# Attention with a mixture-of-experts layer behind it on one Trainium2 core: the same instructions in the order of another scheduler

## The chip, the cores and the metric

The kernel runs on one core of one Trainium2 chip. A core has five engines, each with a queue of its own that it works off strictly in order: TensorE (PE in the profile; its weight loads PEld), VectorE (DVE), ScalarE (ACT), GpSimd (POOL) and SyncE (SP), which here only issues transfers. ACT and POOL issue a few transfers too. The engines wait for each other through semaphores. The metric is the time of one execution on the device in microseconds (us), the median of several runs.

## The reference

```python
scores = scale * np.matmul(q, k.transpose(0, 1, 3, 2))        # 8 batches x 8 heads, 576 positions, 64 dims
mask = block_i >= block_j                                      # causal in blocks of 64
scores = np.where(mask, scores, -1000000000.0)
attn = np.exp(scores - np.max(scores, axis=-1, keepdims=True))
attn = attn / (np.sum(attn, axis=-1, keepdims=True) + 1e-09)
out = np.matmul(attn, v)
x = out.transpose(0, 2, 1, 3).reshape(B * S, H * D)            # 4608 tokens x 512
h = x @ w_in                                                   # 512 x 2048
sp = np.maximum(h, 0.0) + np.log1p(np.exp(-np.abs(h)))         # softplus
g = h * erf(sp)
return (g @ w_out).astype(np.float32)                          # 2048 x 512
```

The weights arrive as float64. The kernel works with pairs of float32r (or float16) numbers, a high and a low part, so a product takes three matmuls.

## The kernel before, in words

The work has two parts that share the engines, and a third behind them.

**Attention** goes over 64 heads (eight batches of eight). For each head, `load_qk` issues four transfers and two subtractions: POOL issues the keys and queries into one of four buffers (L307), SP copies them within the buffer (L308, L309), and POOL subtracts to make the low parts (L312, L313). A buffer is free when PE has done the last matmuls of the head four before. PE makes the scores once for the rows' maxima (L324; DVE reduces them at L327, the maxima go back into the buffer through L354 and L356), once more with keys on partitions (L370, L371); ACT takes the exponential (L375) and the float16 high part (L381), DVE the low part (L382). Every two heads PE multiplies by the values (L414) and makes the sums (L437). Every four heads `normalise` divides (L469 on DVE, L470 on ACT, L471 on POOL) and SP stores the result to a DRAM tensor `x_d` (L472).

**The first part of the MoE layer** takes 6 of the 16 chunks of `d_ff` (128 columns each). It runs over 18 tiles of 256 tokens, three units of two chunks a tile: 54 units. A unit's steps are: the first product on PE (L154, called up here, from the loads of x at L187), the gate `h * erf(softplus(h))` as a polynomial of a tanh (ACT L123 and twice L128, DVE three times L130, then L135, ACT L136, POOL L137), and the second product (L164, called down here). A tile's sums are stored to `part_d` (L210). A tile can start when its batch has gone through all its eight heads, so the first tile stands behind head 7's normalisation. Its six weight chunks are converted from float64 words by `load_weight` (transfer L94; DVE L98, L99, L102, L104, L105; ACT L101, L106; POOL L107, L108) during the first heads, and 110 matmuls that feed nothing (`warm`, L510) stand between those heads. Four more chunks of weights go into the four key buffers as these come free at the end (`early_w2`, eight half-chunks, staged in one buffer for the raw words).

**The second part** (the other 10 chunks) goes over tiles of 512 tokens and adds `part_d`.

The steps are issued by a Python loop over the heads; `merge` spreads the lists of steps of one turn evenly over it. `late` shifts the priority of a kind of steps by a number of instructions:

```python
tc.cur_priority += PRIO.get(kind, 0)
f()
tc.cur_priority -= PRIO.get(kind, 0)
PRIO = {"pv": -74, "w1": 400, "w2": -300}
```

The order in which instructions stand in each engine's queue is not the order of the program. The framework's scheduler makes it: each instruction has a priority, by default its place in the program, and the scheduler picks among those that its model holds ready.

Of the kernel before, what the change touches and what calls it, by code (L numbers as in the profile page):

```python
# [15 lines left out]
AX = mybir.AxisListType  # L16
# the top word of the float64 2**-126, read as a float32
LEAST = 0.25 * (1 + 0.125) * 2.0**-13
PSUM = bass.MemoryType.PSUM

# erf(softplus(h)) as a function of r0 = tanh(T0 * h + T1).  Each step makes the next r:
#   ("S", i):    (p[0] * r_i + p[1]) ** 2
#   ("M", i, j): (r_i + p[0]) * r_j
#   ("A", i, j): p[0] * r_i + r_j
# and the value is the last r plus FIN.
PROG = [('S', 0), ('S', 1), ('M', 2, 2), ('M', 1, 3), ('M', 4, 4)]
# [8 lines left out]
def tile_attention_moe(ctx: ExitStack, tc: tile.TileContext, qk, v, w, maskrows, sels, out):  # L35
    nc = tc.nc
# [52 lines left out]
    def load_weight(whi, wlo, stage, f):  # L89
        """the two float32r parts of chunk f of both weights, out of the words of their float64"""  # L90
        for s in range(2):
            nm = f"{f}_{s}"
            raw = stage[0][0].tile([P, stage[0][2]], I32, tag=stage[0][1][s], bufs=stage[0][3], name=f"raw{nm}")[:, : 2 * DM].rearrange("p (n t) -> p n t", t=2)
            nc.sync.dma_start(raw.rearrange("p n t -> p (n t)"), w[f, s].bitcast(I32))  # L94
            top, low = raw[:, :, 1], raw[:, :, 0]
            # sign, exponent and 20 bits of mantissa as a float32 (0 for what is below its range)
            bits = stage[1][0].tile([P, stage[1][2]], I32, tag=stage[1][1], bufs=stage[1][3], name=f"bits{nm}")[:, :DM]
            nc.vector.tensor_scalar(out=bits, in0=top, scalar1=3, scalar2=0x3FFFFFF8, op0=ALU.logical_shift_left, op1=ALU.bitwise_and)  # L98
            nc.vector.scalar_tensor_tensor(out=bits, in0=top, scalar=-0x40000000, in1=bits, op0=ALU.bitwise_and, op1=ALU.bitwise_or)  # L99
            sq = stage[2][0].tile([P, stage[2][2]], F32, tag=stage[2][1], bufs=stage[2][3], name=f"sq{nm}")[:, :DM]  # L100
            nc.scalar.activation(sq, f32(top), AF.Square)  # L101
            nc.vector.scalar_tensor_tensor(out=sq, in0=sq, scalar=LEAST * LEAST, in1=f32(bits), op0=ALU.is_ge, op1=ALU.mult)  # L102
            # the low word, of the weight that the exponent gives it
            nc.vector.tensor_scalar(out=bits, in0=sq.bitcast(I32), scalar1=-0x800000, scalar2=None, op0=ALU.bitwise_and)  # L104
            nc.vector.scalar_tensor_tensor(out=f32(bits), in0=low.bitcast(U32), scalar=2.0**-52, in1=f32(bits), op0=ALU.mult, op1=ALU.mult)  # L105
            nc.scalar.copy(whi[:, s, :], sq)  # L106
            nc.gpsimd.tensor_tensor(out=sq, in0=sq, in1=f32(whi[:, s, :]), op=ALU.subtract)  # L107
            nc.gpsimd.tensor_tensor(out=wlo[:, s, :], in0=sq, in1=f32(bits), op=ALU.add)  # L108
        return whi, wlo
# [3 lines left out]
    def gate(h, name, gpool):  # L113
        """g = h * erf(softplus(h)) as a sum of two float32r parts"""
        n = h.shape[1]
# [27 lines left out]
    def moe_unit(ws, xh, xl, o, tw, nu, u, name, first, last, spread):  # L143
        """nu chunks of d_ff over tw tokens: the steps to their g, and those to their part of o"""
        turns.append(u)
# [25 lines left out]
    def merged(*lists):  # L171
        """the steps of all lists, each list (steps, from, to) spread evenly over its part of the whole"""
        order = []
        for n, (steps, lo, hi) in enumerate(lists):
            order += [(lo + (hi - lo) * (i + 0.5) / len(steps), n, i) for i in range(len(steps))]
        return [lists[n][0][i] for _, n, i in sorted(order)]
# [4 lines left out]

# [1 line left out]
    def load_x(pool, t, tw):  # L183
# [33 lines left out]
    def moe1(ready, lag):  # L217
        """the next step of the first F1 chunks, if there is one: a unit up to its g together with an earlier unit from g on"""
        t = len(xs1)
# [19 lines left out]
    with tc.tile_pool(name="apool", bufs=2) as apool, tc.tile_pool(name="spool", bufs=1) as spool, \  # L239
# [4 lines left out]
        nc.sync.dma_start(sel, sels)  # L244
        # columns of the keys' tiles 0, 3, 4 and 1, 2 in the two parts of a head's probabilities
        p32s = [spool.tile([P, n], F32, name=f"p32_{i}") for i, n in enumerate(PN)]
# [10 lines left out]
        def bank(name):  # L257
            """a bank of PSUM; all of them take part as long as the other chunks of d_ff need none"""
            turn.append(0)
            k = len(turn) % 8 if not xs1 else 0  # L260
            if k in (2, 5):
                return ps_h.tile([P, 512], F32, tag="h", name=name)
            if k in (3,):
                return ps_o.tile([P, 512], F32, tag="o", name=name)
            return ps_a.tile([P, 512], F32, tag="a", name=name)
# [6 lines left out]
        def prep_v(b, qd, v32):  # L272
            """two float16 parts of v over its largest magnitude, and that magnitude"""
            nm = f"{b}_{qd}"
# [21 lines left out]
        def part(n, i):  # L296
            """part i of head n: kl over kh, qh over ql, kh over 5 rows that mask, qh over 5 rows that mask"""
            return qks[n % NB][:, i * S : (i + 1) * S]
# [18 lines left out]
        def maxes(n):  # L317
            """the steps to the rows' maxima, negated, in the row of t that goes with the ones"""
            mx, K = mxs[n % 2], D + 4
# [41 lines left out]
        def probs(n, out):  # L361
            """the steps to exp(0.125 * s - its maximum), keys on partitions, in two float16 parts"""
            K = D + 5
# [25 lines left out]
        def pv(qd, pp, prs, V, usb, rs):  # L389
            """the steps to the unnormalised outputs of heads 2pp and 2pp+1 of the quad, and to their sums"""  # L390
            vsb, vh, vl = V
            st = {}

            def ranges(q0, q1):
                """keys' tiles that a part of the queries attends to: the queries, and where their probabilities are"""
                for j in range(5):
# [21 lines left out]

            # the sums of two heads' first 384 and last 192 queries, in a group of 32 columns each
            order = []  # L420
# [24 lines left out]
        def normalise(b, qd, usbs, rs):  # L445
            nm = f"{b}_{qd}"
            # pair, tile of the sums, part of the queries, head
            ri = apool.tile([P, 2, 3, 2, 2], F32, tag="ri", name=f"ri{nm}")
# [36 lines left out]
        def late(kind, steps):  # L485
            """steps whose instructions the scheduler holds behind the next ones of the order, or ahead of some (offsets in instructions)"""
            def run(f):
# [69 lines left out]

# [1 line left out]
    N2 = 2  # L559
# [89 lines left out]
```

## Time and profile before

| what | value |
| --- | --- |
| median of 3 runs | 1394.77 us |
| lowest and highest run | 1393.82 and 1400.65 us |
| span of the profiled execution | 1407.0 us |
| mean granted TensorE clock in it | 0.951 |
| busy PE, DVE, ACT, POOL | 1273.8, 1013.9, 793.2, 602.1 us |
| moved by DMA | 179.95 MB |

The profiled execution is one execution of its own, 12.2 us above the median of the runs. An engine counts as busy while it executes an instruction; matmuls are pipelined, and a busy PE is not a PE at its peak. "Idle before" in a group of instructions is the time that the engine stood idle just before them, with the event that ended it behind the arrow. In a timeline each row gives the start, the duration, the engine, the line of the code and the operands; the idle time in front of it stands in brackets.

### The profile page before, as it was taken

The page shows a single profiled execution, that of the slowest core. Times are in us where ns is not written, and L with a number is a line of the kernel's source. Part 1 is how long each engine was busy: PE and PEld are TensorE (multiplying, and loading weights), DVE is VectorE, ACT ScalarE, POOL GpSimd, SP SyncE. Part 2 cuts the span into 40 slices and gives each one's busy share as a digit, 9 for nine tenths or more (in the row PEclk, how much of TensorE's full clock was granted, in tenths as well). Part 3 has the DMA queues.
Part 4 walks back from the last instruction along what each step waited for, and adds up shares of the span by engine and source line. Part 5 has one row for each costly group of instructions (what it writes and reads, how often), then busy time and mean ns, then how long its engine had stood idle before and what let it go on. Part 6 is the DMA issues. An engine that isn't in the chain of part 4 may idle for free. (4 is left out here: it accounts for less than half of the span.)

```text
span 1407.0 us, 21952 instructions
## 1 busy us (share of the span) xinstructions
PE 1273.8 (91%) x8198; PEld 1026.1 (73%) x8198; DVE 1013.9 (72%) x1525; ACT 793.2 (56%) x1493; POOL 602.1 (43%) x454
## 2 busy tenths in 40 slices
PE   3798789989899898999889898779999999999998
PEld 1455567777777787777777787568888888888887
DVE  5768997788878788788697648996555555564654
ACT  1456566667666676667567455544444454445453
POOL 3757665445554554544445424562222222222221
PEclk9879899999999999999999899899999999999999
DMA  8557655757657576566623542302211311321110
GB/s 228 135 125 204 173 156 137 185 154 193 179 129 207 146 196 175 152 161 177 174 81 137 188 164 95 130 0 78 102 60 68 113 60 60 108 72 61 60 61 30
DMA packets 89370, 179.95 MB, mean 128 GB/s; under 512 B 8540, under 2 KB 27292, under 8 KB 89264
## 3 DMA queue, kind: packets, MB, share of 16 engines
q1 hardware_dynamic: 79280, 159.41, 38.1%
q0 software_dynamic: 9344, 18.97, 6.1%
q8 instruction: 65, 1.06, 0.3%
q10 hardware_dynamic: 640, 0.17, 0.1%
q14 instruction: 41, 0.34, 0.1%
HBM read 112.29 MB, written 37.75 MB: 107 GB/s over the span
## 5 line engine op out<-in xcount | busy, mean ns | idle before, releaser
L130 DVE SCALAR_TENSOR_TENSOR m_r<-m_r 128x512 f32<-128x512 f32 x288 | 232.9, 809 | 229.3 <-ACT m_r L128 225.8
L137 POOL TENSOR_TENSOR m_gl<-m_r,m_gh 128x512 fp32r<-128x512 f32 x144 | 195.5, 1357 | 443.7 <-ACT m_gh L136 359.2
L136 ACT CAST m_gh<-m_r 128x512 fp32r<-128x512 f32 x144 | 89.2, 619 | 251.9 <-DVE m_r L135 251.7
L154 PE MATMUL m_h<-xh,whi 128*128 128x256 f32 (+1 forms) x648 | 213.3, 329 | 17.3 <-DVE m_r L135 17.3
L128 ACT ACTIVATE m_r<-m_r,c 128x512 f32<-128x512 f32 x288 | 207.9, 722 | 11.0 <-ACT m_r L128 0.4
L154 PE MATMUL m_h<-xl,whi 128*128 128x256 f32 (+1 forms) x648 | 211.1, 326 | 0.3 <-DMA xl<-x_d 0.3
L154 PE MATMUL m_h<-xh,wlo 128*128 128x256 f32 (+1 forms) x648 | 211.1, 326 | 0.0
L327 DVE TENSOR_REDUCE mx<-s 64x1 f32<-64x288 f32 (+4 forms) x384 | 167.9, 468 | 56.4 <-PE s L324 53.9
L375 ACT ACTIVATE p<-t 128x288 f32<-128x288 f32 (+4 forms) x384 | 143.1, 388 | 97.9 <-PE t L371 76.2
L164 PE MATMUL o<-whi,m_gh 128*128 128x512 f32 x432 | 173.8, 403 | 6.7 <-ACT ob L209 4.3
L164 PE MATMUL o<-wlo,m_gh 128*128 128x512 f32 x432 | 173.8, 402 | 0.0
L382 DVE TENSOR_TENSOR pl<-p,ph 128x832 f16<-128x832 f32 (+1 forms) x128 | 158.5, 1240 | 18.0 <-ACT ph L381 17.8
L312 POOL TENSOR_TENSOR qk<-st,qk 64x576 fp32r<-64x576 f32 x64 | 103.2, 1613 | 157.5 <-PE s L324 55.9
L154 PEld LDWEIGHTS m_h<-xh,whi 128*128 128x128 f32 x648 | 126.6, 195 | 37.8 <-DVE m_r L135 21.9
L164 PE MATMUL o<-whi,m_gl 128*128 128x512 f32 x432 | 153.0, 402 | 0.2 <-POOL m_gl L137 0.2
L370 PE MATMUL t<-qk 69*128 69x288 f32 (+4 forms) x384 | 136.0, 355 | 12.6 <-DVE mx L327 7.0
L324 PE MATMUL s<-qk 68*128 68x256 f32 (+3 forms) x384 | 126.6, 362 | 14.3 <-DVE mx L327 8.7
L313 POOL TENSOR_TENSOR qk<-st,qk 64x576 fp32r<-64x576 f32 x64 | 111.3, 1739 | 65.5 <-DMA qk<-qk 61.7
L154 PEld LDWEIGHTS m_h<-xl,whi 128*128 128x128 f32 x648 | 126.5, 195 | 15.8 <-DMA xl<-x_d 0.6
L154 PEld LDWEIGHTS m_h<-xh,wlo 128*128 128x128 f32 x648 | 126.9, 196 | 9.4
L371 PE MATMUL t<-qk 128*128 128x288 f32 (+4 forms) x384 | 129.8, 339 | 0.0
L123 ACT ACTIVATE m_r<-m_h,c 128x512 f32<-128x512 f32 x144 | 98.8, 686 | 50.5 <-PE m_h L154 48.7
(84 smaller groups left out, 2499.1 us busy)
## 6 DMA issues: line engine op xcount, KB each, us to landing
st<-qk SPq DMA_DIRECT2D x64, 288.0 KB
qk<-qk POOLq DMA_DIRECT2D x64, 288.0 KB, 4.6
qk<-qk SPq DMA_DIRECT2D x64, 288.0 KB
x_d<-xs SPq DMA_DIRECT2D x32, 576.0 KB
raw<-w SPq DMA_DIRECT2D x32, 512.0 KB
v<-v SPq DMA_DIRECT2D x16, 640.0 KB
qk<-qk SPq DMA_DIRECT2D x64, 144.0 KB
xh<-x_d SPq DMA_DIRECT2D x18, 512.0 KB
```

Of the source, the lines that this page charges most:

```text
L128: nc.scalar.activation(r, regs[o[1]], AF.Square, bias=const(pp[1]), scale=pp[0])
L130: nc.vector.scalar_tensor_tensor(out=r, in0=regs[o[1]], scalar=pp[0], in1=regs[o[2]], op0=ALU.add, op1=ALU.mult)
L137: nc.gpsimd.tensor_tensor(out=gl, in0=g, in1=f32(gh), op=ALU.subtract)
L154: nc.tensor.matmul(h[:, k, :], lhsT=a[:, 0, sl], rhs=x[:, cc, :], start=cc == 0 and i == 0, stop=cc == NCC - 1 and i == 2)
L164: nc.tensor.matmul(o[c], lhsT=a[:, sl], rhs=b_[:, 1, :], start=first and k == 0 and not lo and b_ is whi, stop=last and k == nu - 1 and lo)
L313: nc.gpsimd.tensor_tensor(out=t[D:, 1, :], in0=st[D:, :], in1=f32(t[D:, 1, :]), op=ALU.subtract)
L324: nc.tensor.matmul(dst[:r, :w_], lhsT=qh[:K, i * P : i * P + r], rhs=kh[:K, k0 : k0 + w_], start=True, stop=True)
L327: nc.vector.tensor_reduce(out=mx[:r, col : col + 1], in_=src, axis=AX.X, op=ALU.max, negate=True)
L370: nc.tensor.matmul(s[:kk, :w_], lhsT=kh[:K, ks], rhs=qh[:K, q0 : q0 + w_], start=True, stop=False)
L371: nc.tensor.matmul(s[:kk, :w_], lhsT=klh[:, ks], rhs=qhl[:, q0 : q0 + w_], start=False, stop=True)
L375: nc.scalar.activation(p32s[part][:kk, c : c + w_ - skip], s[:kk, skip:w_], AF.Exp, scale=SCALE)
L382: nc.vector.tensor_tensor(out=pl, in0=p, in1=ph, op=ALU.subtract)
```

## The change

Comments and docstrings are taken out (they are blank lines now, so the line numbers stay), and the framework's context is made with one more argument:

```diff
-    with tile.TileContext(nc) as tc:
+    with tile.TileContext(nc, schedule_with_timeline_sim=True) as tc:
```

With it the scheduler orders the instructions by a simulation of the timeline in place of its usual model. Instructions, buffers and operands are the same; the order on each engine is another one, and with it the places at which the engines wait for each other. Of the 64 heads, those from 11 on show most of it on PE and POOL.

On POOL, around the loads of heads 26 to 28 (buffers `qk2`, `qk3`, `qk0`), there stood before:

```order
L307 DMA qk2_96<-qk 64x2x576
L312 TENSOR_TENSOR qk2_96<-st_26_3210,qk2_96 64x576
L137 TENSOR_TENSOR m1_2_1_gl_8457<-m1_2_1_r1_8459,m1_2_1_gh_8456 128x512
L313 TENSOR_TENSOR qk2_96<-st_26_3210,qk2_96 64x576
L307 DMA qk3_97<-qk 64x2x576
L312 TENSOR_TENSOR qk3_97<-st_27_3306,qk3_97 64x576
L307 DMA qk0_94<-qk 64x2x576
L313 TENSOR_TENSOR qk3_97<-st_27_3306,qk3_97 64x576
L137 TENSOR_TENSOR m1_2_2_gl_8505<-m1_2_2_r1_8507,m1_2_2_gh_8504 128x512
```

and there stands now:

```order
L137 TENSOR_TENSOR m1_3_2_gl_8661<-m1_3_2_r1_8663,m1_3_2_gh_8660 128x512
L307 DMA qk2_96<-qk 64x2x576
L312 TENSOR_TENSOR qk2_96<-st_26_3210,qk2_96 64x576
L313 TENSOR_TENSOR qk2_96<-st_26_3210,qk2_96 64x576
L307 DMA qk3_97<-qk 64x2x576
L312 TENSOR_TENSOR qk3_97<-st_27_3306,qk3_97 64x576
L313 TENSOR_TENSOR qk3_97<-st_27_3306,qk3_97 64x576
L307 DMA qk0_94<-qk 64x2x576
```

The gates' last step (L137, `m1_tile_unit`) has gone from inside a load to the place between two, and head 28's L307 from ahead of head 27's L313 to behind it; over heads 4 to 63 such an L307 stood ahead of the previous L313 17 times and does 3 times, and of the L137 that lie between two loads or inside one, from head 11 on, 4 of 32 stood between an L313 and the next L307 with no load open, and 31 of 39 do now.

On PE, between the scores of heads 20 and 21 (`t2_20`, `t0_21`), there stood before:

```order
L371 MATMUL t2_20_256_2929<-qk0_94 128x320
L324 MATMUL s01_23_2945<-qk3_97 128x256 x2
L370 MATMUL t0_21_0_2950<-qk1_95 128x288
L414 LDWEIGHTS vh2_0_2127
L414 MATMUL u4_1_1_2954<-ph0_18_2659,vh2_0_2127 64x320
```

and there stands now, with some of unit 2_0's down matmuls (`o1_2_0`) and half of unit 3_0's up matmuls between the two heads, of which these are the first:

```order
L371 MATMUL t2_20_256_2929<-qk0_94 128x320
L324 MATMUL s01_23_2945<-qk3_97 128x256 x2
L154 MATMUL m1_2_2_h_8475<-xh256_512_2760,whi5_1301 128x256
L154 MATMUL m1_2_2_h_8475<-xl256_512_2762,whi5_1301 128x256
L154 MATMUL m1_2_2_h_8475<-xh256_512_2760,wlo5_1302 128x256
L164 MATMUL o1_2_0_8163<-whi0_321,m1_2_0_gh_8335 128x512
L164 MATMUL o1_2_0_8163<-wlo0_322,m1_2_0_gh_8335 128x512
L154 MATMUL m1_3_0_h_8519<-xh256_768_7257,whi0_321 128x256
```

Six units stand close together in heads 11 to 14, 19 to 22, 27 to 30, 43 to 46, 51 to 54 and 58 to 62, nine in heads 35 to 39, and the heads between have none; they were spread over all heads from 11 on, about three units to four heads. Nineteen units stood behind head 63, and nine do now (tiles 15 to 17).

On DVE, at heads 62 and 63, with the conversion of weights into freed buffers between (`bits7_1` is of the fourth half-chunk, `bits8_0` and `bits8_1` of the fifth and sixth), there stood before:

```order
L382 TENSOR_TENSOR pl0_62_7986<-p32_0_113,ph0_62_7985 128x832
L130 SCALAR_TENSOR_TENSOR m1_11_2_r1_9959<-m1_11_2_r1_9959 128x512
L98 TENSOR_SCALAR bits7_1_8269<-raw7_1_8267 128x512
L382 TENSOR_TENSOR pl1_62_8033<-p32_1_114,ph1_62_8032 128x768
L99 SCALAR_TENSOR_TENSOR bits7_1_8269<-raw7_1_8267,bits7_1_8269 128x512
L130 SCALAR_TENSOR_TENSOR m1_11_2_r1_9959<-m1_11_2_r0_9958,m1_11_2_r1_9959 128x512
L102 SCALAR_TENSOR_TENSOR sq7_1_8272<-sq7_1_8272,bits7_1_8269 128x512
L130 SCALAR_TENSOR_TENSOR m1_11_2_r1_9959<-m1_11_2_r1_9959 128x512
L104 TENSOR_SCALAR bits7_1_8269<-sq7_1_8272 128x512
L382 TENSOR_TENSOR pl0_63_8067<-p32_0_113,ph0_63_8066 128x832
L105 SCALAR_TENSOR_TENSOR bits7_1_8269<-raw7_1_8267,bits7_1_8269 128x512
L382 TENSOR_TENSOR pl1_63_8098<-p32_1_114,ph1_63_8097 128x768
```

and there stands now:

```order
L382 TENSOR_TENSOR pl0_62_7986<-p32_0_113,ph0_62_7985 128x832
L135 SCALAR_TENSOR_TENSOR m1_14_2_r1_10445<-m1_14_2_r1_10445,m1_14_2_h_10401 128x512
L98 TENSOR_SCALAR bits8_0_8351<-raw8_0_8349 128x512
L99 SCALAR_TENSOR_TENSOR bits8_0_8351<-raw8_0_8349,bits8_0_8351 128x512
L102 SCALAR_TENSOR_TENSOR sq8_0_8354<-sq8_0_8354,bits8_0_8351 128x512
L104 TENSOR_SCALAR bits8_0_8351<-sq8_0_8354 128x512
L382 TENSOR_TENSOR pl1_62_8033<-p32_1_114,ph1_62_8032 128x768
L105 SCALAR_TENSOR_TENSOR bits8_0_8351<-raw8_0_8349,bits8_0_8351 128x512
L98 TENSOR_SCALAR bits8_1_8364<-raw8_1_8362 128x512
L382 TENSOR_TENSOR pl0_63_8067<-p32_0_113,ph0_63_8066 128x832
L99 SCALAR_TENSOR_TENSOR bits8_1_8364<-raw8_1_8362,bits8_1_8364 128x512
L382 TENSOR_TENSOR pl1_63_8098<-p32_1_114,ph1_63_8097 128x768
```

Head 63's last subtraction has moved from behind the fourth half-chunk to behind the start of the sixth.

Three more places have moved. The conversion of the first weights stands ahead of the end of head 1 on DVE (it was spread to head 11), and the 110 warming matmuls ahead of head 2 on PE. Between a unit's last up matmul and its first down matmul PE's order holds less other work than before. The second MoE part is in practically the same order.

## The prediction

> **What bounds the kernel now.** I read the busy time by stage first, then the groups of instructions, then the queue of GpSimd (POOL), whose loads set the pace of the heads. The windows give for each stage its length and each engine's busy time, then TensorE's (PE's) granted clock. By the order they are heads 0 to 10, heads 11 to 63, the rest of the first MoE part, the conversion of weights, and the second MoE part.
>
> ```profile
> PE 33%; DVE 6%; issue 2%; ACT 1%; POOL 0%; DVEq 0%; POOLq 0%; ACTq 0%
> ```
> ```profile
> core 0: us, PE busy (x) PEld busy (x) DVE busy (x) ACT busy (x) POOL busy (x), PEclk, DMA share, GB/s
> 0.00:161.20 161.20, 116.48 (x751) 72.04 (x751) 121.70 (x202) 75.07 (x160) 100.19 (x89) 0.85 0.67 175
> 161.20:751.90 590.70, 538.88 (x4560) 441.85 (x4559) 482.90 (x770) 401.36 (x844) 302.02 (x221) 0.96 0.61 163
> 751.90:852.00 100.10, 92.35 (x588) 79.95 (x589) 61.14 (x83) 50.76 (x84) 36.79 (x26) 0.95 0.44 152
> 852.00:954.50 102.50, 77.95 (x327) 61.46 (x326) 97.75 (x112) 50.78 (x81) 56.49 (x37) 0.87 0.22 75
> 954.50:1407.00 452.50, 448.08 (x1977) 370.85 (x1975) 250.41 (x362) 215.22 (x324) 106.63 (x83) 1.00 0.21 72
> ```
>
> The chain that ended last (first fence) is mostly PE, since its last 450 us have PE busy at 448 of 452.5; in the stage before, DVE is busy 97.75 of 102.5. In the largest stage 53 heads take 590.7 us, 11.15 us each, and no engine is full there: PE is the busiest, and a busy PE there includes matmuls that wait in its pipe. What a head waits for stands in POOL's queue:
>
> ```profile
> L313 POOL TENSOR_TENSOR qk<-st,qk 64x576 fp32r<-64x576 f32 x64 | 111.3, 1739 | 65.5 <-DMA qk<-qk 61.7 <-DMA part_d<-ob 1.0 <-ACT p L375 0.7
> L307 POOL DMA_DIRECT2D qk<-qk x64 | 39.5, 618 | 59.3 <-PE s L324 19.8 <-PE t L371 17.9 <-PE m_h L154 11.4
> ```
> ```profile
> qk<-qk POOLq DMA_DIRECT2D x64, 288.0 KB, 4.6
> ```
> ```profile
> 382.06 0.62 POOL L307 DMA_DIRECT2D qk<-qk  x1 [1.14 <-PE m_h L154]
> 388.04 1.41 POOL L312 TENSOR_TENSOR qk<-st,qk 64x576 fp32r<-64x576 f32 x1 [5.37 <-PE s L324]
> 391.14 1.73 POOL L313 TENSOR_TENSOR qk<-st,qk 64x576 fp32r<-64x576 f32 x1 [1.68 <-DMA qk<-qk]
> ...
> 404.18 1.75 POOL L313 TENSOR_TENSOR qk<-st,qk 64x576 fp32r<-64x576 f32 x1
> 405.87 0.62 POOL L307 DMA_DIRECT2D qk<-qk  x1
> 406.59 1.29 POOL L137 TENSOR_TENSOR m_gl<-m_r,m_gh 128x512 fp32r<-128x512 f32 x1
> 411.17 1.40 POOL L312 TENSOR_TENSOR qk<-st,qk 64x576 fp32r<-64x576 f32 x1 [3.30 <-PE t L371]
> 414.27 1.43 POOL L313 TENSOR_TENSOR qk<-st,qk 64x576 fp32r<-64x576 f32 x1 [1.70 <-DMA qk<-qk]
> 415.65 0.61 POOL L307 DMA_DIRECT2D qk<-qk  x1
> ```
>
> A head's keys and queries are issued by L307, land 4.6 us later, are copied by two transfers of SyncE, and reduced by L312 and L313. From L307's start to L313's end that is 10.8 us for the first load shown (382.06 to 392.87) and 9.8 for the other (405.87 to 415.70), and at 405.87 and 415.65 the next L307 starts the moment the L313 ahead of it ends. Where L307 stands behind the previous head's L313 in POOL's queue, one load cannot begin until the last is finished, and the loads run at about 10.2 us a head: the chain just under the 11.15. It goes faster where two loads overlap, as here, where the L307 at 356.57 starts 3.0 us ahead of the end of the L313 at 358.19:
>
> ```profile
> 346.80 0.61 POOL L307 DMA_DIRECT2D qk<-qk  x1
> ...
> 356.57 0.62 POOL L307 DMA_DIRECT2D qk<-qk  x1
> 358.19 1.42 POOL L313 TENSOR_TENSOR qk<-st,qk 64x576 fp32r<-64x576 f32 x1 [0.99 <-DMA part_d<-ob]
> ```
>
> There are four buffers, so loads lead the heads, and a long head is partly paid back by short ones. These are the last subtractions of the probabilities of heads 37 to 40:
>
> ```profile
> 459.62 0.96 DVE L382 TENSOR_TENSOR pl<-p,ph 128x768 f16<-128x768 f32 x1 [0.89 <-ACT ph L381]
> 480.00 1.42 DVE L382 TENSOR_TENSOR pl<-p,ph 128x768 f16<-128x768 f32 x1
> 488.55 0.95 DVE L382 TENSOR_TENSOR pl<-p,ph 128x768 f16<-128x768 f32 x1
> 495.64 0.96 DVE L382 TENSOR_TENSOR pl<-p,ph 128x768 f16<-128x768 f32 x1 [0.98 <-ACT ph L381]
> ```
>
> After 20.4 us come 8.55 and 7.09, 7.8 in the mean: two heads at which the lead was used up.
>
> **The change, part by part.** No instruction is added or removed; the sum is of moved work alone. Four stages differ.
>
> A. *Heads 11 to 58: MoE units in bursts.* In the order before, the units of the first MoE part are spread, about one tile of three units per four heads. Now they stand in bursts as soon as a batch's rows are written: six units in four heads (nine in five at heads 35 to 39), then heads with attention alone. The price of a unit is read from the tail, where little else runs:
>
> ```profile
> 817.37 0.37 SPq L187 DMA_DIRECT2D xh<-x_d  x1
> ...
> 835.05 0.39 SPq L187 DMA_DIRECT2D xh<-x_d  x1
> ```
>
> These loads of x start each time a tile's buffers come free: 17.7 us a tile of three units, 5.9 a unit. A unit has 24 matmuls of 256 columns and 12 of 512, 12,288 columns, so PE does 2,083 columns per us there. A head's scores (twice 1,856 columns and 1,984) are 5,696 columns and its products some 3,200 where two halves or four quarters of the array are taken to run side by side: 8,900 columns, 4.3 us, 4.4 with the transposes. So a burst of four heads costs PE 6 x 5.9 + 4 x 4.4 = 53 us, against 44.6 at 11.15 a head. With q for a quiet head's time, a batch of eight heads is 53 + 4q against 89.2, and the batch of nine units 75 + 3q; five of the one and one of the other change the stage by 23q - 195 us. A quiet head needs little of PE and is bound by its load: q lies between 7.8 (the give-back) and 10.2 (the chain). POOL's order decides: a load stood ahead of the previous L313 for 17 of 60 heads and does for 3 now, so most quiet heads go at 10.2 once the lead is refilled. A burst leaves the lead full (the loads ran on meanwhile, up to the four buffers), which pays two heads of four: q = 9.0, and 23q - 195 = +12.
>
> To this come stalls of PE within the bursts. A unit's second product needs its gate, which is long:
>
> ```profile
> L130 DVE SCALAR_TENSOR_TENSOR m_r<-m_r 128x512 f32<-128x512 f32 x288 | 232.9, 809 | 229.3 <-ACT m_r L128 225.8
> L137 POOL TENSOR_TENSOR m_gl<-m_r,m_gh 128x512 fp32r<-128x512 f32 x144 | 195.5, 1357 | 443.7 <-ACT m_gh L136 359.2
> L136 ACT CAST m_gh<-m_r 128x512 fp32r<-128x512 f32 x144 | 89.2, 619 | 251.9 <-DVE m_r L135 251.7
> L128 ACT ACTIVATE m_r<-m_r,c 128x512 f32<-128x512 f32 x288 | 207.9, 722 | 11.0 <-ACT m_r L128 0.4
> L123 ACT ACTIVATE m_r<-m_h,c 128x512 f32<-128x512 f32 x144 | 98.8, 686 | 50.5 <-PE m_h L154 48.7
> ```
> ```profile
> L135 DVE SCALAR_TENSOR_TENSOR m_r<-m_r,m_h 128x512 f32<-128x512 f32 x144 | 98.4, 684 | 4.7 <-DVE m_r L130 0.5
> ```
>
> 0.69 + 2 x 0.72 + 3 x 0.81 + 0.68 + 0.62 + 1.36 = 7.2 us with no queueing. Between a unit's last up matmul and its first down matmul the order before has 20 to 30 us of PE work; now 7 to 16, and 7 to 9 for the last units of a burst, with the heads' own DVE and ACT work in the gate's way. I take one stall of 4 us a burst (bounds 0 and 8): 6 x 4 = +24. A is +36.
>
> The gates' L137 now stand mostly between an L313 and the next L307, 31 of 39 against 4 of 32; each holds the next load up by its 1.36 us, but only inside bursts, where PE is the limit and the 53 us hide it; without that cover it would be 31 x 1.36, some 42 us.
>
> B. *The start.* All of the first weights' conversion now stands ahead of head 1's end on DVE, and all 110 warming matmuls ahead of head 2's; both were spread to head 10. The first heads begin later and the next ones have less in the way; loads at 10.2 a head set the rest of the stage. DVE is busy 121.70 of its 161.20 us, so the work fits: 0, bounds -10 and +10.
>
> C. *The last heads.* The second subtraction of head 63 stood on DVE behind the fourth half-chunk of weights that goes into freed buffers, and stands behind the start of the sixth now.
>
> ```profile
> L382 DVE TENSOR_TENSOR pl<-p,ph x11: 943/1011/2284, 699.8 to 751.0; 128x768 f16<-128x768 f32 x6, 128x832 f16<-128x832 f32 x5
> ```
> ```profile
> L105 DVE SCALAR_TENSOR_TENSOR bits<-raw,bits x8: 672/686/1780, 716.4 to 792.5; 128x512 f32<-128x512 uint32 x8
> ```
>
> Eight halves take 7 steps in 76.1 us, 10.9 each (one staging buffer). Heads 58 to 63 took 51.2 us. One and a half steps more is +16; I take +15, since DVE and PE have other work in that time, bounds +10 and +20.
>
> D. *The rest of the first MoE part.* After head 63 there stood 19 units, now nine (tiles 15 to 17). Their rows must be written, loaded and used:
>
> ```profile
> 149.21 0.38 SPq L472 DMA_DIRECT2D x_d<-xs  x1
> ```
> ```profile
> L154 PE MATMUL m_h<-xh,whi x648: 274/283/796, 160.8 to 1387.7; 128*128 128x256 f32 x108, 128*128 128x512 f32 x54
> ```
> ```profile
> 766.11 2.20 SPq L472 DMA_DIRECT2D x_d<-xs  x2
> ```
>
> The first batch's last store of x went out at 149.21 and the first MoE matmul began at 160.8: 11.6 us. Head 63 ends at 752 and its last store is at 766.11 + 2.20 = 768, 16 us later. Before, ten more units stood ahead of tile 15, whose turn came at 817.4, 65.4 us after head 63. Now nothing does: 16 + 11.6 + some 4 us to fill the empty pipe = 32, which is -33 (bounds -38 and -28). From there on the orders are the same, conversion and second MoE part too: 0.
>
> Sum: 36 + 0 + 15 - 33 = +18, 1.3% on the profiled execution of 1407.0 us. That execution is 12 us above the median of the runs, 1394.8; I apply the difference to the median: 1412 us. The measurement tells about 0.5% (7 us) from no change.
>
> [...]
>
> In the first window the clock is 0.85, with PE busy 116 of 161 us. [...]
>
> **The rivals.**
> 1. *Elastic: the lead absorbs the bursts* (faster). Loads go on during a burst, so more than two quiet heads run at the give-back pace: q = 8.0, and gates find DVE and ACT less loaded, stalls of 2 us: 23 x 8.0 - 195 + 12 = +1. Then 1 + 15 - 33 = -17: 1378 us. For it: 8.55 and 7.09 after a long head. Against: 3 overlapped loads where there were 17. It decides at q under 8.2 with stalls of 4, or under 9.3 with none.
> 2. *Rigid: nothing is paid back.* L137 and L471 in front of L307 use up the lead within the burst: q = 10.2, stalls of 6: 40 + 36 = +76, and +58 in all: 1452 us. For it: 31 of 39 gates now stand in the load's way. Against: a burst's 13.3 us a head leave 3 us of room for each load.
> 3. *The terms cancel.* A is +18 (q = 9.0, stalls of 1): 1395 us, within 0.5%.
>
> **How the numbers follow.** Forecast 0.35 (1402 to 1435 by itself), elastic 0.28, rigid 0.17, cancelling 0.20. Slower by over 0.5% is forecast and rigid, 0.52; same 0.20; faster 0.28. The range goes from 1368 (elastic, with the better end of B) to 1455 (rigid), since both sides hold too much to leave out.
>
> **What would show it.** In the trace after: bursts of 13 us a head or more followed by heads of 8 to 10 us; POOL's L307 starting right at the end of an L313 in quiet heads; more idle time of PE put down to DVE or POOL ahead of the down matmuls L164; head 58 to 63 near 66 us; tile 15's loads some 32 us after head 63; the second MoE part still 452 us. I am wrong if q is 8 or the bursts run without stalls, or if the first 161 us move by more than 10.

## The result: 9.5% slower

The changed kernel takes 1532.53 us (median of 4 runs, 1525.45 to 1535.82) against 1396.06 us before (4 runs). The ratio is 1.0954, 95% interval 1.0915 to 1.0994. The prediction had the sign right (1412 us) and the size wrong: 136 us came in place of 18, beyond the upper end of its range at 1455. The profiled execution has a span of 1532.6 us against 1407.0. Of the runs below, the second of r16_fill_overlap, 1710.06 us at a granted clock of 0.724, was in a slower state than all others and is left out.

### The profile page after: what moved, and what is told of

The parts are those of the page before. It is cut to its first block, busy times and chain, and to the rows that moved or that the text cites. A ratio compares the mean times of both kernels' runs of the same rounds, so it can differ in the third digit from the quotient of the medians.

```text
span 1532.6 us, 21888 instructions
## 1 busy us (share of the span) xinstructions
PE 1341.0 (87%) x8198; PEld 1071.4 (70%) x8198; DVE 1013.4 (66%) x1525; ACT 788.8 (51%) x1493; POOL 596.8 (39%) x454
## 5 line engine op out<-in xcount | busy, mean ns | idle before, releaser
L130 DVE SCALAR_TENSOR_TENSOR m_r<-m_r 128x512 f32<-128x512 f32 x288 | 236.6, 823 | 228.7 <-ACT m_r L128 225.4
L137 POOL TENSOR_TENSOR m_gl<-m_r,m_gh 128x512 fp32r<-128x512 f32 x144 | 195.1, 1356 | 438.6 <-ACT m_gh L136 414.8
L154 PE MATMUL m_h<-xh,whi 128*128 128x256 f32 (+1 forms) x648 | 213.3, 331 | 73.9 <-DMA xh<-x_d 60.7
L312 POOL TENSOR_TENSOR qk<-st,qk 64x576 fp32r<-64x576 f32 x64 | 99.3, 1552 | 198.1 <-PE t L371 60.2
L164 PE MATMUL o<-whi,m_gh 128*128 128x512 f32 x432 | 171.0, 396 | 4.3 <-ACT m_gh L136 4.1
L382 DVE TENSOR_TENSOR pl<-p,ph 128x832 f16<-128x832 f32 (+1 forms) x128 | 149.1, 1165 | 35.5 <-ACT ph L381 34.6
L164 PE MATMUL o<-wlo,m_gh 128*128 128x512 f32 x432 | 170.9, 396 | 0.0
L370 PE MATMUL t<-qk 69*128 69x288 f32 (+4 forms) x384 | 153.5, 400 | 17.9 <-DVE mx L327 5.9
L313 POOL TENSOR_TENSOR qk<-st,qk 64x576 fp32r<-64x576 f32 x64 | 107.1, 1675 | 128.0 <-DMA qk<-qk 124.8
L324 PE MATMUL s<-qk 68*128 68x256 f32 (+3 forms) x384 | 141.2, 405 | 10.6 <-DVE mx L327 5.3
L164 PE MATMUL o<-whi,m_gl 128*128 128x512 f32 x432 | 138.2, 394 | 4.0 <-POOL m_gl L137 4.0
L371 PE MATMUL t<-qk 128*128 128x288 f32 (+4 forms) x384 | 137.6, 359 | 0.0
```

The source lines that it names most:

```text
L130: nc.vector.scalar_tensor_tensor(out=r, in0=regs[o[1]], scalar=pp[0], in1=regs[o[2]], op0=ALU.add, op1=ALU.mult)
L137: nc.gpsimd.tensor_tensor(out=gl, in0=g, in1=f32(gh), op=ALU.subtract)
L154: nc.tensor.matmul(h[:, k, :], lhsT=a[:, 0, sl], rhs=x[:, cc, :], start=cc == 0 and i == 0, stop=cc == NCC - 1 and i == 2)
L164: nc.tensor.matmul(o[c], lhsT=a[:, sl], rhs=b_[:, 1, :], start=first and k == 0 and not lo and b_ is whi, stop=last and k == nu - 1 and lo)
L313: nc.gpsimd.tensor_tensor(out=t[D:, 1, :], in0=st[D:, :], in1=f32(t[D:, 1, :]), op=ALU.subtract)
L324: nc.tensor.matmul(dst[:r, :w_], lhsT=qh[:K, i * P : i * P + r], rhs=kh[:K, k0 : k0 + w_], start=True, stop=True)
```

## The profile after

The windows again, first of the kernel before and then of the changed one, cut at the same places: the end of head 10, of head 58, of head 63 (each taken at the head's last L382) and the end.

```profile
0.00:161.00 161.00, 116.28 (x751) 71.90 (x751) 121.51 (x202) 75.07 (x160) 100.19 (x89) 0.85 0.67 175
161.00:702.00 541.00, 494.52 (x4191) 406.21 (x4192) 439.37 (x705) 366.41 (x770) 276.91 (x205) 0.96 0.63 168
702.00:752.00 50.00, 44.66 (x372) 35.86 (x370) 43.82 (x67) 34.94 (x74) 25.21 (x16) 0.97 0.34 106
752.00:1407.00 655.00, 618.29 (x2890) 512.16 (x2889) 409.20 (x554) 316.76 (x489) 199.82 (x145) 0.97 0.25 85
```
```profile
0.00:173.00 173.00, 126.74 (x754) 83.06 (x754) 135.00 (x210) 77.78 (x162) 108.04 (x93) 0.76 0.60 156
173.00:849.00 676.00, 585.33 (x4369) 468.45 (x4369) 441.66 (x720) 383.43 (x793) 271.79 (x207) 0.85 0.52 137
849.00:931.00 82.00, 70.89 (x528) 57.90 (x528) 60.02 (x85) 47.05 (x97) 33.93 (x23) 0.88 0.36 109
931.00:1532.60 601.60, 558.01 (x2553) 462.01 (x2547) 376.69 (x511) 280.54 (x441) 183.07 (x131) 0.96 0.25 85
```

The stages changed by +12, +135, +32 and -53 us, 126 in all. Heads 11 to 58 carry it. DVE, ACT and POOL are busy there for nearly the same time as before; PE is busy 91 us longer, at a granted clock (the column after POOL) of 0.85 in place of 0.96. Here is one batch of eight heads (19 to 26) in pieces, most of them one head long:

```profile
282.00:293.00 11.00, 5.11 (x36) 3.69 (x37) 0.05 (x1) 0.88 (x2) 1.39 (x1) 0.53 1.06 299
293.00:305.00 12.00, 11.40 (x87) 9.96 (x86) 9.03 (x16) 8.63 (x20) 2.53 (x3) 1.00 0.39 92
305.00:315.00 10.00, 9.28 (x96) 7.91 (x97) 7.43 (x12) 5.67 (x13) 6.86 (x5) 1.00 0.37 83
...
345.00:353.00 8.00, 7.24 (x88) 5.74 (x87) 5.21 (x9) 6.56 (x14) 0.62 (x1) 1.00 0.66 189
353.00:362.00 9.00, 6.23 (x27) 3.89 (x25) 6.02 (x11) 4.30 (x10) 3.36 (x3) 0.76 0.41 92
362.00:370.00 8.00, 8.00 (x84) 6.34 (x83) 5.73 (x9) 4.88 (x12) 3.27 (x3) 0.63 0.42 92
370.00:381.00 11.00, 9.97 (x53) 7.07 (x53) 8.41 (x15) 7.19 (x16) 4.85 (x5) 0.72 0.56 128
381.00:392.00 11.00, 7.87 (x56) 5.51 (x52) 8.42 (x15) 6.11 (x12) 5.82 (x4) 0.50 0.71 201
```

The burst of six units takes 71 us (282 to 353) and the four quiet heads 39. In the first 11 us of the burst PE is busy 5 at a clock of 0.53 while the transfers run at 299 GB/s; from 293 on it is busy at full clock; in the quiet heads it is busy most of the time again, at 0.50 to 0.76. The first 11 us in PE's timeline, and SyncE's queue at that place:

```profile
278.63 0.63 PE L324 MATMUL s<-qk 68*128 68x256 f32 x2
287.89 0.80 PE L154 MATMUL m_h<-xh,whi 128*128 128x256 f32 x2 [8.64 <-DMA xh<-x_d]
288.49 0.44 PE L370 MATMUL t<-qk 69*128 69x288 f32 x1
```
```profile
279.12 0.38 SPq L472 DMA_DIRECT2D x_d<-xs  x1
281.26 0.35 SPq L306 DMA_DIRECT2D st<-qk  x1
282.05 0.36 SPq L187 DMA_DIRECT2D xh<-x_d  x1
282.47 0.50 SPq L187 DMA_DIRECT2D xl<-x_d  x1
283.01 0.51 SPq L187 DMA_DIRECT2D xh<-x_d  x1
283.56 0.52 SPq L187 DMA_DIRECT2D xl<-x_d  x1
284.18 2.35 SPq L269 DMA_DIRECT2D v<-v  x1
```

The first MoE matmul of the batch stands in PE's queue ahead of head 19's scores (L370), and PE waits 8.6 us for x, which is loaded behind the last store of x (L472), with the scores behind it. In all of the trace, and in the last line for heads 11 to 58 alone:

```profile
PE m_h L154 <- DMA xh<-x_d: 60.7, 8, 12.5
PE o L164 <- ACT m_gh L136: 4.1, 3, 1.6
PE o L164 <- POOL m_gl L137: 4.0, 3, 1.5
POOL qk L313 <- DMA qk<-qk: 124.8, 50, 10.3
DVE vm L276 <- DMA v<-v: 45.4, 13, 12.9
PE m_h L154 <- DMA xh<-x_d: 41.7, 6, 8.6
```

Before, PE waited for x for under 1 us in all; POOL's wait ahead of L313 was 61.7 us, and DVE's for the values stood so:

```profile
DVE vm L276 <- DMA v<-v: 18.9, 6, 9.9
```

The stalls behind the gates that the prediction feared (L164) are 8 us.

## An account of PE's time

In these traces the clock's record has two values, full and half, in pieces of 3.41 us or a multiple of it (the longest in the trace before is 471 us). In the trace before, matmuls of 512 columns (L164) start every 0.23 us at full clock and every 0.43 at half (797 to 806 us, around a change of the clock at 804). So PE's time can be split: *idle* is the time in which no matmul record is open, *half-clock loss* is half of the busy time at half clock, and *work* is what is left. By definition the three make the span. What is not by definition is that the work comes out the same in every kernel with the same instructions (1201 to 1218 us in whole executions), however they are ordered; the two kernels with fillers have some 60 more.

| kernel | median, us | span | work | idle | half-clock loss |
| --- | --- | --- | --- | --- | --- |
| before | 1396.1 | 1407 | 1213 | 133 | 61 |
| changed | 1532.5 | 1533 | 1203 | 192 | 138 |
| r1_spread | 1499.1 | 1498 | 1205 | 168 | 125 |
| r6_before_burst | 1626.4 | 1625 | 1210 | 244 | 171 |
| r2_later | 1528.5 | 1527 | 1201 | 195 | 130 |
| r8_sp | 1498.0 | 1495 | 1203 | 167 | 125 |
| r7_later_sp | 1502.8 | 1502 | 1202 | 177 | 123 |
| r9_spread_sp | 1490.3 | 1484 | 1208 | 165 | 111 |
| r3_fill | 1511.5 | 1513 | 1267 | 156 | 89 |
| r4_overlap | 1506.2 | 1501 | 1202 | 160 | 139 |
| r16_fill_overlap | 1499.8 (one run) | 1498 | 1270 | 144 | 83 |
| r10_pe_of_before | 1472.3 | 1469 | 1217 | 175 | 77 |
| r11_rest_of_before | 1535.5 | 1533 | 1211 | 170 | 152 |
| r12_before_pe_of_after | 1553.5 | 1545 | 1204 | 188 | 152 |
| r13_pe_pool_sp | 1439.4 | 1438 | 1218 | 146 | 74 |
| r14_pe_dve_act | 1428.9 | 1426 | 1212 | 152 | 61 |
| r15_spread_sp_overlap | 1474.2 | 1476 | 1209 | 156 | 112 |
| r5b_before_overlap | 1370.5 | 1375 | 1213 | 110 | 53 |

The changed kernel has 59 us more idle time and 77 us more half-clock loss, less 10 of work: the 126 us. In heads 11 to 58 alone the 135 us are 31 of work (units that the bursts drew forward from the tail), 44 idle and 60 half-clock loss. With 471 us of work in 541, PE had little room in those heads before.

The split says where PE's time went, not what it would save if a part were gone. Cut at the ends of the bursts, the same heads of the changed kernel hold:

| heads 11 to 58, changed | span | work | idle | half-clock loss |
| --- | --- | --- | --- | --- |
| six bursts | 453 | 383 | 51 | 19 |
| 23 quiet heads | 223 | 119 | 40 | 64 |

So 64 of the 83 us of half-clock loss stand in the quiet heads, and only 19 in the bursts. Of the 51 us idle in the bursts, 42 are the waits for x, of 5.2 to 8.6 us each.

## The experiments

All edits but the matmuls added in r3_fill and r16_fill_overlap fix orders by edges without a wait (`add_manual_dep(later, earlier.name, NoSync)`): the later instruction stands behind the earlier one in the same engine's queue. The diffs are shortened: `...` stands for code left out, `NOSYNC` for the edge without a wait, and comments are added. The kernel before took 1392 to 1399 us beside each group of runs.

What an edge leaves free, the scheduler orders anew, so hardly any run differs from its base in the named place alone. Counted by the names in the traces, as what lies outside the longest common order, at least 472 of PE's 8198 instructions, 94 of DVE's 1525 and 33 of SyncE's 435 stand elsewhere in r8_sp than in the changed kernel, and 639, 140 and 44 in r4_overlap. What such a run gains is the work of the edit and of this new order together.

**The place of the units on PE.** *r1_spread* ties each unit of tiles 1 to 12 behind the head at which it stood before; *r6_before_burst* does the reverse under the usual scheduler.

```diff
+    AT = {'m1_1_0': (13, 17), 'm1_1_1': (15, 18), ...}   # head ahead of the up matmuls, of the down matmuls
-        return ([lambda k=k, cs=cs: up(k, cs) for k ...
+        return ([lambda k=k, cs=cs: at(hu, up, k, cs) for k ...   # at: with tc.issue_after(last_t[hu])
```

> The changed kernel with one thing undone: each MoE unit of tiles 1 to 12 is tied on PE (order only, no wait) behind the scores of the head at which it stood in the order before, so that no unit can be drawn forward into a burst. Everything else is left to the timeline scheduler. Theory 1 (the bursts are the loss: heads without MoE run at a low clock, and PE stands at each burst's first unit): heads 11 to 58 come back to about 11 us each, clock about 0.95, 1395 to 1430 us. Theory 2 (the loads of keys and queries, one behind the other on POOL, are the loss whatever PE does): 1500 us or more. Theory 3 (it is the start and the last heads): 1515 us or more, since those are left as they are.

> The kernel before, usual scheduler, with the MoE units of tiles 1 to 14 held on PE, from both sides, at the heads at which the changed kernel has them; all other orders are the usual scheduler's own. Theory 1 (the bursts are the loss): six batches of eight heads at about 110 us in place of 89, 1490 to 1530 us, clock about 0.89. Theory 2 (the order of the loads on POOL): 1395 to 1420 us, since the loads keep the usual scheduler's order. If both count, in between, about 1450.

r1_spread took 1499.07 us, r6_before_burst 1626.44. So the bursts are a cause: undone they give back 33 us, and made on top of the usual scheduler they cost 232, more than the whole change. The window of heads 11 to 58 of r6_before_burst shows it as the changed kernel does, only worse:

```profile
156.00:924.00 768.00, 632.55 (x4355) 503.69 (x4354) 434.69 (x730) 392.91 (x794) 267.02 (x211) 0.78 0.44 120
```

But theory 1 alone falls too: with the units spread 1499 us remain where it expected 1430 at most. And in the changed kernel, with other orders on all queues, bursts at the same heads come with less (1533 against 1626).

**The wait for x.** *r2_later* ties each batch's first tile, from head 19 on, one head later on PE, so that scores stand where PE waited. *r8_sp* puts no edge on PE and moves the values' transfer ahead of the first x, and the second tile's x behind the next head's copies; *r7_later_sp* does both, and *r9_spread_sp* does it with the spread units.

```diff
+    XBEHIND[t0] = lambda b_=b_: [vload[2 * b_ + 4]] ...          # first tile of a batch: behind the values
+    XBEHIND[t1] = lambda b_=b_: [copied[min(8 * b_ + 14, 63)]]   # second tile: behind the next head's copies
```

> The changed kernel with the first tile of each batch from head 16 on tied one head later on PE (order only), so that PE does a head's scores while x lands, in place of standing at the burst's first matmul, which took 48 us of idle time in the trace of the changed kernel. If that wait is a loss of its own: 48 us less, about 1485. If PE would wait for the heads' loads anyway, or the clock is what costs: 1520 to 1535.

> The changed kernel with each batch's first tile tied one head later on PE, as in the second kernel of the runs before, which gained nothing: its trace shows the wait gone from the first MoE matmul and come back at DVE, which stands 7 to 9 us at the reduction of the values, whose transfer is issued behind four transfers of x. Now SyncE's order is changed too (order only): the values' transfer ahead of the first x, and the second tile's x behind the next head's copies. Theory 4 (the crowd of transfers at a burst's start, some 3 MB in 10 us, is what stops the engines): 6 x 8 us less, about 1480. Theory 1 with the clock alone: 1520 to 1530. If the loads of the heads bound it: 1520 or more.

> The changed kernel with SyncE's order alone changed (values' transfer ahead of the first x, second tile's x behind the next head's copies), PE's order left. Theory 4: x lands earlier and alone, the wait at the burst's first matmul falls from 8 to 4 us, 1500 to 1510. If the place of the units on PE is what matters: 1525 to 1535.

> The changed kernel with the MoE units spread as in the order before (the first kernel of the runs before: 1499 us, heads 11 to 58 at 13.0 us, clock 0.86 there) and SyncE's order changed as in the two kernels beside it. Theory 4: DVE's waits for the values, 31 us in that trace, go: 1465 to 1475. If the rest of the loss is in the loads' order on POOL or in the heads' own order: 1495 to 1500.

r2_later took 1528.47 us, no change that could be told. Its waits for x fell from 60.7 to 11.7 us, and others stood up in their place (L366 here is L354 in the changed kernel, where that wait was 13.2 us):

```profile
PE mt L366 <- DVE mx L364: 61.2, 13, 14.0
PE m_h L160 <- DMA xh<-x_d: 11.7, 2, 11.3
```
```profile
283.88 1.55 DVE L339 TENSOR_REDUCE mx<-s 128x1 f32<-128x384 f32 x3
293.21 1.49 DVE L288 TENSOR_REDUCE vm<-v 128x1 f32<-128x1280 f32 x1 [7.78 <-DMA v<-v]
294.62 0.44 DVE L339 TENSOR_REDUCE mx<-s 64x1 f32<-64x288 f32 x1
```

Here DVE stands 7.8 us at the reduction of the values (L288), whose transfer is issued behind four of x, and the maxima (L339) stand behind it, for which PE waits. DVE's waits for the values are 65.8 us in all there, against 45.4. With SyncE's order changed, r8_sp took 1497.98 and r7_later_sp 1502.75. The wait for x in r8_sp shrank:

```profile
PE m_h L154 <- DMA xh<-x_d: 40.4, 8, 11.0
```

So taking the transfers at a burst's start apart gives some 30 us; once they are apart, the place of the first matmul makes no difference (1498 and 1503). Theory 4's 8 us a burst are 4 to 6. r9_spread_sp took 1490.26, 9 us less than r1_spread, between the two answers that were expected.

**The clock and the loads.** *r3_fill* adds 12 matmuls a head that feed nothing to the quiet heads. *r4_overlap* ties L313 of each head behind the L307 of the next, and *r16_fill_overlap* does both.

```diff
+                for _ in range(2 if n >= 11 and n % 8 in (7, 0, 1, 2) and n < 59 else 0):
+                    nc.tensor.matmul(s, lhsT=ident16, rhs=ident16[:, None, :].broadcast_to([P, 4, P]), start=True, stop=True)
```
```diff
-                nc.gpsimd.dma_start(t[:D, 2:4, :], qk[b, h] ...
+                ld = nc.gpsimd.dma_start(t[:D, 2:4, :], qk[b, h] ...
+                if n - 1 in lows:
+                    tc.add_manual_dep(lows[n - 1], ld.ins.name, NOSYNC, reason="order")
-                nc.gpsimd.tensor_tensor(out=t[D:, 1, :], ...
+                lows[n] = nc.gpsimd.tensor_tensor(out=t[D:, 1, :], ...
```

> The changed kernel with 12 matmuls a head that feed nothing (their bank is overwritten by the scores) in the four quiet heads of every eight, 11 to 58, 2.6 us of PE each at full clock, to hold the clock up. Theory 1a (the low clock, 0.65 in the quiet heads, is what makes 39 us of four quiet heads): the clock there rises to 0.9 or more, four quiet heads take 32 to 36 us, and the whole 1490 to 1510. If the loads bound the quiet heads: 1525 to 1540 at a higher clock. If PE is the bound there at any clock: 1560 or more.

> The changed kernel with the last step of each head's load (L313) tied behind the next head's issue (L307) on POOL, so that two loads always overlap. Theory 2 (loads one behind the other are what bounds the quiet heads and keeps the lead from filling): quiet heads at 8 us or less in place of 9.8, 24 x 2 = 48 us less, 1480. If PE at half clock bounds the quiet heads: 1520 to 1535.

> The changed kernel with both the fillers in the quiet heads (12 matmuls a head that feed nothing) and the loads made to overlap. If half clock and the serial loads are two limits at the same height, each hidden behind the other: four quiet heads in 32 to 36 us in place of 39, the whole 1460 to 1485. If something else bounds the quiet heads: 39 us again, 1490 to 1505.

r3_fill took 1511.53 us. It adds 64 us of work to PE and is 21 us faster: half-clock loss falls by 49 us and idle time by 36. r4_overlap took 1506.16: 26 us faster, with 32 less idle time and the half-clock loss unchanged. Both lie between the answers that were expected. In neither do the quiet heads get shorter. Heads 23 to 26 of the changed kernel and of r3_fill:

```profile
353.00:392.00 39.00, 32.06 (x214) 22.82 (x212) 28.58 (x47) 22.48 (x49) 17.30 (x14) 0.65 0.54 133
```
```profile
349.00:388.00 39.00, 34.64 (x275) 23.69 (x276) 26.47 (x47) 23.11 (x51) 19.41 (x14) 0.96 0.60 154
```

They take 39 us at a clock of 0.96 as at 0.65, and 39 us in r4_overlap. All 23 quiet heads take 246 us in r3_fill and 228 in r4_overlap, against 223 in the changed kernel; it is the bursts that are shorter, 425 and 430 us against 453. There PE's wait for x is smaller. In heads 11 to 58 of r3_fill it is

```profile
PE m_h L154 <- DMA xh<-x_d: 11.3, 4, 5.0
```

where the changed kernel has 41.7 us, and in all of r4_overlap 17.7 where it has 60.7. SyncE's queue has the stores and loads of x at the bursts in another order in both runs. So neither run shows that the low clock, or the order of the loads, is what costs the time: the gain stands where the wait for x stood, and what part the clock or the loads have in it stays open.

In r16_fill_overlap four quiet heads take 35 to 39 us, and the whole 1499.77 us, inside what was expected if something else bounds the quiet heads. All its quiet heads take 217 us against 228 in r4_overlap, with 65 us more work on PE: a hint, from one execution, that the low clock costs something there once the loads overlap. The fillers themselves are 10 us of PE in four heads (48 matmuls, at the 216 ns from start to start that the warming matmuls of the kernel before have at full clock), so this run does not settle what bounds a quiet head when neither clock nor loads do; that stays open.

**Whole queues.** A table of positions fixes every instruction of the named engines in the order of one kernel, and the scheduler orders the other engines around it.

In outline:

```diff
+    for engine, order in ORDERS.items():
+        mine = [i for i in traced if str(i.engine) == engine]
+        for a, b in zip(order, order[1:]):
+            tc.add_manual_dep(mine[b], mine[a].name, NOSYNC, reason="order")
```

> The timeline scheduler with PE's whole order fixed to that of the kernel before (a table of positions, order only); the other four engines are ordered by the timeline scheduler around it. Theory 5 (by the account of PE's time in the runs so far, span = work + idle + half-clock loss, the loss is PE's idle time and the low clock that follows it, made by the order on PE alone): 1395 to 1420, clock about 0.95. If the order on the other engines carries it, since PE waits for them: 1470 or more.

> The other way round: DVE, ACT, POOL and SyncE fixed to the order of the kernel before, PE ordered by the timeline scheduler around them. Theory 5: 1470 or more, since PE's order is still the new one (though it must follow the others' order). If the others carry it: 1395 to 1430.

> The usual scheduler with PE's whole order fixed to that of the changed kernel, the other engines ordered by the usual scheduler around it. Theory 5: 1500 to 1560, clock 0.88. If the others carry it: 1395 to 1430. The kernel with the MoE units alone held at the changed kernel's heads under the usual scheduler took 1626, so more than 1560 would say that the usual scheduler does worse with PE's order than the timeline scheduler.

> The timeline scheduler with the orders of PE, POOL and SyncE fixed to those of the kernel before; DVE and ACT are ordered by the timeline scheduler. If the transfers' issue (loads one behind the other on POOL, x ahead of the values on SyncE) carries the 72 us left: 1395 to 1415. If the order on DVE and ACT carries it: 1460 or more.

> The timeline scheduler with the orders of PE, DVE and ACT fixed to those of the kernel before; POOL and SyncE are ordered by the timeline scheduler. If the transfers' issue carries the 72 us left: 1455 or more. If DVE and ACT carry it (the values' reduction ahead of the maxima): 1395 to 1415.

| order of the kernel before on | the rest by | median, us | ratio, 95% interval |
| --- | --- | --- | --- |
| none | timeline simulation | 1532.5 | 1.0915 to 1.0994 |
| PE | timeline simulation | 1472.3 | 1.0487 to 1.0571 |
| PE, POOL, SyncE | timeline simulation | 1439.4 | 1.0245 to 1.0379 |
| PE, DVE, ACT | timeline simulation | 1428.9 | 1.0170 to 1.0304 |
| DVE, ACT, POOL, SyncE | timeline simulation | 1535.5 | 1.0943 to 1.1020 |

With PE's old order 60 us come back and 73 remain. Theory 5, by which the order on PE alone makes the loss, falls with that. With all the other engines' old order and PE left to the timeline simulation nothing comes back (1535.54 us); PE's order there is a third one, with 2094 of its 8198 instructions elsewhere than in the changed kernel. r12_before_pe_of_after, the usual scheduler around exactly PE's new order, ends at 1553.47. So PE's new order is enough for the whole loss, with what that scheduler makes of the other queues around it. It is not needed for all of it: of the 73 to 76 us that remain with PE's old order, fixing the transfers' queues takes 33 away and fixing DVE and ACT 43, each between the two answers that were expected. Set against the kernel before of its own group (1399.40 and 1393.93) each run is 73, 45 and 35 us over, and the two shares are 27 and 38. With PE's old order, DVE still stands 43.7 us at the values:

```profile
DVE vm L315 <- DMA v<-v: 43.7, 12, 8.4
POOL qk L352 <- DMA qk<-qk: 95.1, 52, 11.5
```

against 18.9 and 61.7 us before (there L276 and L313). With POOL and SyncE fixed as well, DVE's wait is 25.1 us, with DVE and ACT fixed 28.5.

**A kernel that beats both.** *r5_before_overlap* is the kernel before, usual scheduler, with the edge of r4_overlap; *r5b_before_overlap* is the same kernel measured again, *r15_spread_sp_overlap* has that edge on top of r9_spread_sp.

> The kernel before, usual scheduler, with each head's last load step (L313) tied behind the next head's issue (L307) on POOL, so that two loads always overlap (17 of 60 do in the order before). If the loads bound the heads in the kernel before, as the prediction had it: 1350 to 1375. If PE is the bound (471 us of work at full clock in 541 us of heads 11 to 58): 1385 to 1400.

> The usual scheduler with the loads made to overlap, again: 1368 to 1378, 1.3 to 2.2% below the kernel before.

> The changed kernel with the units spread, SyncE's order changed (1490 in the run before) and the loads made to overlap as well. If the loads' order on POOL is what is left: 1440 or less. If the order on DVE and ACT, and the start (168 us against 161), are: 1475 to 1490.

r5_before_overlap took 1373.62 us and r5b_before_overlap 1370.48 (6 runs), a ratio of 0.9806 to the kernel before, interval 0.9765 to 0.9847. That is what was expected if the loads bound the heads of the kernel before, and below the 1385 us that PE as the bound would have allowed. The loads overlap at all heads, a load takes longer (13.2 us a head in the mean against 10.6), and POOL's wait for the copies ahead of the last step falls from 61.7 to 21.7 us (L316 here is L313 before). The second line is the window of heads 11 to 58:

```profile
L316 POOL TENSOR_TENSOR qk<-st,qk 64x576 fp32r<-64x576 f32 x64 | 100.6, 1571 | 25.2 <-DMA qk<-qk 21.7
```
```profile
160.00:686.00 526.00, 500.24 (x4253) 410.83 (x4253) 419.47 (x714) 365.63 (x776) 279.77 (x209) 0.96 0.64 174
```

Heads 11 to 58 take 526 us in place of 541, with 26 us idle in place of 46, and PE is busy 500 of the 526. The other orders moved here too (179 of DVE's 1525 instructions, 62 of SyncE's 435), so the gain is measured, and the overlap as its cause is argued. r15_spread_sp_overlap took 1474.20, 16 us less than r9_spread_sp and just under the 1475 to 1490 expected if the loads are not what is left: in the timeline's order they are not the main thing.

## Why the prediction was wrong

The bursts cost far more than their term, and a part of the loss hangs on queues for which the sum had no term.

- *Step A, the burst (53 us of PE and 4 of stall)* is the term that failed. The five bursts of six units took 71 to 74 us and that of nine 91 against 79, 89 us more in all than the 364 forecast. Of these, 43 are work that was priced too low: the sum had 340 us of PE for the bursts, and they hold 383. Some 20 of them are the price of an attention head: the 23 quiet heads, which hold no unit, have 119 us of full-clock work, 5.2 each and not 4.4. What the other 23 are stays open. Another 27 are idle time: 51 us where 24 were allowed for stalls. And 19 are half clock. The wait for x, 5.2 to 8.6 us at each burst's start and 42 us in heads 11 to 58, was not in the sum at all.
- *Gate stalls of 24 us* named the wrong wait: 8 us came, and the wait for x in their place.
- *The quiet heads* took 223 us where q = 9.0 gives 207: q was 9.7, inside the bounds of 7.8 and 10.2, and POOL's L307 starts as the L313 ahead of it ends, as forecast:

```profile
358.37 1.41 POOL L313 TENSOR_TENSOR qk<-st,qk 64x576 fp32r<-64x576 f32 x1 [2.06 <-DMA qk<-qk]
359.73 0.61 POOL L307 DMA_DIRECT2D qk<-qk  x1
```

- *"No engine is full there"* was half right. Heads 11 to 58 held 471 us of full-clock work in 541, so PE had less room than the forecast gave it; but the loads did bound a part of these heads, as the forecast had it, for the kernel before got faster with overlapped loads.
- *The half clock* has no term in the sum. Half-clock loss grew by 77 us: 53 in the quiet heads, 7 in the bursts, 15 in the start, and 2 in the rest. What the 53 cost no run settles: r3_fill's quiet heads were no shorter at a higher clock (heads 23 to 26: 39 us at 0.96 as at 0.65).
- *That only PE's and POOL's queues matter* was wrong: with PE's old order 33 us hang on POOL's and SyncE's orders and 43 on DVE's and ACT's (27 and 38 by each group's own kernel before). The order of x and the values on SyncE alone was worth some 30 us in r8_sp. The forecast gave these no term.
- *B* was 0 and came out at +12, half-clock loss 15 more and work 4 less. The first weights' conversion, which now holds back DVE, and the warming matmuls, used up by head 2, are the likely reasons; no run tests them.
- *C* was +15 and came out at +32: 20 of it is work drawn forward, the rest idle time and clock.
- *D* was -33 and came out at -53, with 57 less work, which was done earlier; tile 15's first product began 21 us behind head 63, where 32 was forecast, 4 of them an estimate that no run shows. C and D belong together, as their errors nearly cancel: -21 for the -18 forecast. The 31 us of work in A belongs to them too: drawing work forward gains little where PE has little room.
- *The rivals:* none of them had the mechanism. The rigid one (1452) had the sign, and its q of 10.2 is as far from 9.7 as the forecast's is; it put the loss on POOL's L137, which no run tests by itself.
- *The second MoE part unchanged* was right: 452 us in both.

## What to carry to other kernels

Before moving work between stages, split the bounding engine's time into work, idle and clock loss: an engine at 87% real work (here 471 of 541 us) has little room to give. But look at where the lost clock stands before calling it a cost: four quiet heads took 39 us at a clock of 0.96 as at 0.65. Here a wait that was removed was taken over by the next operand of the same crowd of transfers (r2_later against the changed kernel: PE's for x from 60.7 to 11.7 us, DVE's for the values from 45.4 to 65.8), so treat the crowd, not the wait. Fixing an engine's whole order, and letting a scheduler fill in the rest, tells in a few runs which queue a loss hangs on; with a few edges alone, compare the free queues too, for the scheduler moves them.

## What the runs showed of the hardware

In these traces the clock of TensorE stood at full or half in pieces of 3.41 us or a multiple of it; the trace before has 139 us at half in all, the changed one 356. At the start of the burst shown PE waits 8.6 us for x, and the clock is 0.53 over those 11 us (282 to 293).

A busy PE was not enough for the full clock: in the start of the changed kernel PE is busy 25.3 of 26 us, with the clock (the third figure from the end) at half throughout, and what holds it there no run shows:

```profile
106.00:132.00 26.00, 25.34 (x146) 19.55 (x144) 12.48 (x27) 13.27 (x31) 11.02 (x9) 0.50 0.43 111
```

Unexpected was that 64 us of work for nothing made a kernel faster by 21 us, with a new order of the rest, and that PE's full-clock work came out within 17 us (1.4%) over sixteen orders of the same instructions.
